# Block sums of the mixing matrix made in DRAM by copies and adding transfers, and weight pieces split three steps earlier, in a two-layer attention and gMLP kernel

## The chip, the cores and the metric

The kernel runs on one core of a Trainium2 chip. The metric is the device time of one execution in microseconds. The core has engines with queues of their own: TensorE (PE; its weight loads are shown as PEld), VectorE (DVE), ScalarE (ACT), GpSimd (POOL) and SyncE (SP), which here issues every transfer. Sixteen transfer engines move data between DRAM, where inputs, output and scratch tensors lie, and the on-chip memory.

## The reference

Two pairs of layers run over x (2048 rows of 512). The first of a pair is linear attention with 32 heads of 16, the second a gMLP block whose mixing matrix w_sp (2048 x 2048) mixes rows:

```python
x = x + A(layernorm(x)); x = x + B(layernorm(x)); x = x + A(layernorm(x)); x = x + B(layernorm(x))

def A(x, wqkv, wo):      # per head, phi(t) = where(t > 0, t + 1, exp(t)) + 1e-6
    kv = einsum("bhsd,bhse->bhde", phi(k), v);  z = einsum("bhsd->bhd", phi(k))
    return (phi(q) @ kv / (phi(q) . z + 1e-6)) @ wo

def B(x, w_in, w_sp, b_sp, w_out):
    z = gelu(x @ w_in)                       # 1792 wide, halves z1 and z2 of 896
    g = einsum("ts,bsf->btf", w_sp, layernorm(z2)) + b_sp
    return (z1 * g) @ w_out
```

All is float32. The same weights serve both pairs, so w_sp is used twice.

## The kernel before

Every large product runs as three TensorE passes on split operands: `high` (ScalarE) rounds an operand, `low` (VectorE) makes the rest, `mm3` multiplies high by high, high by low and low by high. A matmul has a 128 x 128 weight and 512 columns, or 448 in one product.

Each of two layers L has three stages.

P1 (`P1.run`, steps s = 1 to 17, "the first half" in the short description of the change) goes over 16 row tiles of 128 rows: normalise (`ln_a`, `ln_b`), turn by a round trip through DRAM or by TensorE (`Turn`), the K projection, for s up to 10 the Q projection too (the last six Q tiles come later), phi (`phi`, its last operation on VectorE is L329), and the product `Gmm`, 12 matmuls each. `K_split` (L341) makes the operand of `Gmm`. Beside that, seven pieces of the weight `win2` are split, one a step: `side[0].fetch()` loads a piece from s = 6 on and `side.popleft().piece()` splits it from s = 7 on (to 13), with one ScalarE and one VectorE operation on tiles named bg.

P2 (`P2.run`, steps s = 1 to 18) finishes attention and starts the gMLP. In a step it makes the attention output of a tile (`c`), adds it to x, takes row statistics (`stats`: VectorE sums, then three small POOL operations L200, L201, L203), normalises (ScalarE, L209), stores and reloads the tile turned (tensors yt; qt is the same for queries), projects it onto win2 (`e`, 24 matmuls of 448 columns), and projects groups of four tiles onto win1 (`f`, stored to DRAM as z1). `w1.piece(True)` splits pieces of win1, with the low part on POOL, in the first steps.

P4 (`P4.run`) applies w_sp by a Strassen-like scheme of seven products in the order P2, P1, P6, P7, P4, P5, P3, each in 8 steps k over blocks (56 steps g in all, 24 matmuls in a step of P2, P1, P4 and P5, 18 in the others; lines L902 to L904). Step g calls `fetch(g + 4)`, which loads its w_sp blocks, two 128 x 512 sheets, into a quad buffer, and `sp(g + 2)`, which splits them (L840 on ScalarE, L841 on VectorE). P6, P7, P5 and P3 use not blocks of w_sp but sums of blocks. With a21, a22, a11, a12 for four sheets of one (k, j) there are four sums: s1 = a21 + a22, s3 = a21 + a11, s2 = s1 + a11, s4 = s2 + a12. They are the same in both layers, so they are made once, in layer 0, and kept in DRAM: `Sums.s[m, k]`, a pair of sheets j = 0, 1.

Class `Sums` makes them in 32 ticks of two POOL adds each (L782). A tick stores the sheets of the tick before (`store`, L777), loads sheets for the next (`fetch`, three or one of them, L115 through `load`), and adds. Four ticks run in P1 of layer 0 (steps 2 to 5, in sheets cut from two big buffers by class `Sheets`), the others in P2 from step 6 on and in P4 up to step 15 (`if s > 5: sums.tick()`, `if g < 16: self.sums.tick()`). In layer 1 there is nothing left to do for a tick. All loads and stores go through SP's queue in program order; a store that waits for its data holds those behind it. The order of every queue is written out by hand: it is the order of the calls.

Of the kernel before, what the change touches and what calls it, by code (L numbers as in the profile page):

```python
# [10 lines left out]
F32 = mybir.dt.float32  # L11
# [4 lines left out]
P = 128  # L16
# [13 lines left out]
class Slots:  # L30


    def __init__(self, pool, prefix, n):
        self.pool, self.prefix = pool, prefix
        self.free_list = deque(range(n))
        self.held = {}
        self.count = 0
# [9 lines left out]
    def put(self, *tiles):  # L47
        for t in tiles:
            n, _ = self.held.pop(id(t))
            self.free_list.append(n)  # L50


class Sheets:


    def __init__(self, slots, n):
        self.slots = slots
        self.tiles = [slots.get([P, NF, 512]) for _ in range(n)]
        self.free_list = deque(t[:, f, :] for t in self.tiles for f in range(NF))

    def get(self, shape):
        return self.free_list.popleft()

    def put(self, *sheets):
        self.free_list.extend(sheets)

    def close(self):
        self.slots.put(*self.tiles)


@with_exitstack
def mixer_kernel(ctx: ExitStack, tc: tile.TileContext, x_in, wqkv, wo_d, win1_d, win2_d, wsp_d, bsp_d, wout_d,
# [192 lines left out]
    class P1:  # L265
# [163 lines left out]
        def run(self, sums):  # L429
            side = deque([self.win2] * NF)  # L430
            ND = NT - DEFER
            for s in range(1, NT + 2):
                self.loadx(s + 3)
                self.turn.load(s + 1)
                if 2 <= s < NT:
                    self.T_high(s)
                if s == 1:
                    if not self.kb:
                        self.K(0)
                    self.K(1)  # L440
                elif 2 < s <= NT:
                    self.K(s - 1)
                self.ln_a(s + 2)
                if 2 <= s < NT:
                    self.T_low(s)
                if s <= NT:
                    self.K_phi(s - 1)
                if s <= ND:
                    self.Q(s - 1)
                if s == NT + 1:  # L450
                    self.late()
                if s <= NT:
                    self.xsplit(s - 1)
                    self.K_split(s - 1)
                self.ln_b(s + 2)
                if s <= ND:
                    self.Q_phi(s - 1)
                if s >= 2:
                    self.Gmm(s - 2)
                if s == NT + 1:  # L460
                    self.late_phi()
                if self.L == 0 and s == 2:
                    sums.slots = Sheets(bigs, 2)
                if self.L == 0 and 2 <= s < 6:
                    sums.tick(s < 5)
                if self.L == 0 and s == 6:
                    sums.store()
                    sums.slots.close()
                    sums.slots = pages
                if s == 6:  # L470
                    self.wv, self.wo = (quads.get([P, 4, 512]) for _ in range(2))
                    nc.sync.dma_start(self.wv, wqkv[:, 1024:1536].rearrange("(c p) f -> p c f", p=P))
                    nc.sync.dma_start(self.wo, wo_d.rearrange("(c p) f -> p c f", p=P))
                if s > 6 and side:
                    side.popleft().piece()
                if s > 5 and side:
                    side[0].fetch()


# [62 lines left out]
    class P2:  # L542
# [152 lines left out]
        def run(self, sums):  # L695
            w1 = self.win1
            for s in range(1, NT + 3):
                self.loadx(s + 1)
                self.qturn.load(s + 1)
                if s in self.qturn.by_pe:  # L700
                    self.c(s - 1)
                    self.b_high(s)
                    self.c2(s - 1)
                    self.b_low(s)
                    if s >= 2:
                        self.d_high(s - 2)
                        self.d_low(s - 2)
                    self.p1.late()
                    self.c3(s - 1)
                    self.a2(s + 2)  # L710
                    self.p1.late_phi()
                    self.a(s + 3)
                else:
                    if s < NT:
                        self.b_high(s)
                    self.a2_den(s + 2)
                    if s < NT:
                        self.b_low(s)
                    if s <= NT:
                        self.c(s - 1)  # L720
                        self.c2(s - 1)
                    if s == NT:
                        quads.put(*self.W2)
                        pages.put(self.zbc)
                    self.a2_mul(s + 2)
                    late = s - 2 in self.xturn.by_pe
                    if late:
                        self.d_high(s - 2)
                        self.d_low(s - 2)
                    if s <= NT:  # L730
                        self.c3(s - 1)
                    self.a(s + 3)
                    if s <= NT + 1 and not late:
                        self.d_high(s - 2)
                        self.d_low(s - 2)
                if s >= 4:
                    self.e4(s - 4)
                self.xturn.load(s - 1)
                if s >= 3:
                    self.e(s - 3)  # L740
                    self.e2(s - 3)
                    self.e3(s - 3)
                self.f()
                self.f()
                self.fq.extend(self.fnext)
                self.fnext = []
                w1.piece(True)
                w1.fetch()
                if s > 5:
                    sums.tick()  # L750
                if s >= NT + 1:
                    self.p4.fetch(s - NT - 1)
            self.e4(NT - 1)
            self.win2.free()


    class Sums:

        def __init__(self):
            self.s = {(m, k): dram.tile([P, 2, 512], F32, name=f"s{m}_{k}") for m in range(1, 5) for k in range(HT)}
            self.todo = deque((k, j, h) for k in range(HT) for j in range(2) for h in range(2))
            self.ahead = deque(self.todo)
            self.raw, self.made, self.done = {}, [], []
            self.slots = pages

        def fetch(self):
            if self.ahead:
                k, j, h = self.ahead.popleft()  # L770
                at = ((j, k), (j, k + HT), (2 + j, k)) if h == 0 else ((2 + j, k + HT),)
                self.raw.setdefault((k, j), []).extend(load(wsp_d[n, s], self.slots) for n, s in at)

        def store(self):

            for m, k, j, t in self.made:
                nc.sync.dma_start(self.s[m, k][:, j, :], t)  # L777
            self.slots.put(*self.done)
            self.made, self.done = [], []

        def add(self, m, k, j, t, a, b):
            nc.gpsimd.tensor_tensor(t, a, b, op=OP.add)  # L782
            self.made.append((m, k, j, t))

        def tick(self, ahead=True):
            self.store()
            if not self.todo:
                return
            if not self.raw:
                self.fetch()  # L790
            if ahead or self.todo[0][2] == 0:
                self.fetch()
            k, j, h = self.todo.popleft()
            if h == 0:
                a21, a22, a11 = self.raw[k, j][:3]
                self.add(1, k, j, a22, a21, a22)
                self.add(3, k, j, a21, a21, a11)
                self.done = [a21]
            else:
                _, a22, a11, a12 = self.raw.pop((k, j))  # L800
                self.add(2, k, j, a11, a22, a11)
                self.add(4, k, j, a12, a11, a12)
                self.done = [a22, a11, a12]


    class P4:
# [15 lines left out]
        def fetch(self, g):  # L822
            if g >= len(self.steps):
                return
            p, k = self.steps[g]
            t = quads.get([P, 2, 512])
            if p in ("P1", "P2", "P4"):
                n, s = {"P1": (2, k), "P2": (2, k + HT), "P4": (0, k + HT)}[p]
                nc.sync.dma_start(t, wsp_d[n:n + 2, s].rearrange("j p t -> p j t"))
            else:  # L830
                nc.sync.dma_start(t, self.sums.s[{"P6": 2, "P7": 3, "P5": 1, "P3": 4}[p], k])
            self.raw[g] = t

        def sp(self, g):
# [169 lines left out]
        def run(self, nxt):  # L1004
# [10 lines left out]
            for g in range(n):  # L1015
# [6 lines left out]
                if evac_first:  # L1022
                    self.evac(p)
                    self.sp(g + 2)
                if g < 16:
                    self.sums.tick()
                if g == 3:
                    self.loadb()
# [86 lines left out]
```

## Time and profile before

| | us |
|---|---|
| median of 3 runs | 1404.9 (1404.71 to 1405.46) |
| the profiled execution | 1404.73 |
| its span, first to last instruction | 1402.9 |
| busy in the span: TensorE, VectorE, ScalarE, POOL | 1389.6, 886.4, 561.0, 405.6 |

The page of the profile gives busy times by engine, the chain of work that ended last, and groups of instructions by line, each with count, busy time, mean length and idle time of the engine just before it, with what ended that. Other views group by stretches of time ("windows": busy time and count of each engine, granted TensorE clock, share of the 16 transfer engines in use, GB/s), list waits by who waited for whom, or list instructions in order of time. A matmul's row lasts longer than the interval to the next, since they overlap. The granted clock is 1.00 throughout. Line numbers are those of the kernel before.

These groups are POOL's largest, beside the two that the prediction shows: the gates of P4 (L929, 85.5 us), the running sum of phi(k) (L346, 48.8 us), and the three operations of the row statistics (L200, L201, L203: 36.4, 54.8 and 27.2 us).

### The profile page before, as it was taken

Reading aid. Unit: us, or ns where it says so; the run is one execution under the profiler, and the core shown is the slowest. Engines: PE = TensorE matmul, PEld = TensorE weight load, DVE = VectorE, ACT = ScalarE, POOL = GpSimd, SP = SyncE. Lnnn points to the kernel's source line nnn. Section 1 sums busy time; section 2 is a strip of 40 time slices with the busy share of each in tenths; the row PEclk is TensorE's granted clock in tenths of the full one; section 3 lists DMA queues with packets and bytes.
Section 4 is the critical chain, followed back from the end, with each engine's and each line's share of the span. In section 5 each row is a group of like instructions: output and inputs, shape, how many; then the busy total and the mean of one; then the engine's idle time right before and its main releaser. Section 6 shows DMA issues by size and latency. Waiting matters only on the chain.

```text
span 1402.9 us, 17320 instructions
## 1 busy us (share of the span) xinstructions
PE 1389.6 (99%) x6230; PEld 1156.7 (82%) x6230; DVE 886.4 (63%) x1251; ACT 561.0 (40%) x847; POOL 405.6 (29%) x490
## 2 busy tenths in 40 slices
PE   9999999999999999999999999999999999999998
PEld 7877788888888888888788778888888888888887
DVE  7786777752577666573577867766415466665632
ACT  5564534434323332341356645444333233333420
POOL 4644345544365002040023434432100030022300
PEclk9999999999999999999999999999999999999999
DMA  5842267876897433443635413555334344334432
GB/s 176 270 142 62 73 192 237 271 228 207 305 326 248 134 120 135 173 158 120 210 101 184 129 46 99 179 179 162 114 116 158 104 165 134 133 117 167 155 110 94
DMA packets 142263, 225.69 MB, mean 161 GB/s; under 512 B 11744, under 2 KB 50400, under 8 KB 142176
## 3 DMA queue, kind: packets, MB, share of 16 engines
q1 hardware_dynamic: 142176, 224.57, 48.6%
q8 instruction: 49, 0.80, 0.2%
q14 instruction: 38, 0.31, 0.1%
HBM read 156.63 MB, written 67.90 MB: 160 GB/s over the span
## 4 chain that ended last, share of the span: by engine, by line
PE 87%; DVE 6%; ACT 4%; issue 1%; DMA 1%; POOL 0%; SPq 0%; DVEq 0%; ACTq 0%; POOLq 0%
PE bank L135 15%; PE bank L134 15%; PE bank L133 15%; PE bank L902 13%; PE bank L904 13%; PE bank L903 13%; DVE pg L260 1%; DVE pg L341 1%; DVE pg L329 1%; ACT pg L328 1%; DMA pg<-in_win_dram 1%; ACT pg L327 1%; PE bank L515 1%; PE bank L526 0%; PE bank L221 0%
## 5 line engine op out<-in xcount | busy, mean ns | idle before, releaser
L902 PE MATMUL bank<-qd,pg 128*128 128x512 f32 x800 | 311.2, 389 | 0.0
L904 PE MATMUL bank<-qd,pg 128*128 128x512 f32 x800 | 311.2, 389 | 0.0
L903 PE MATMUL bank<-qd,pg 128*128 128x512 f32 x800 | 311.2, 389 | 0.0
L841 DVE TENSOR_TENSOR qd<-qd,qd 128x1024 fp32r<-128x1024 f32 x112 | 151.8, 1355 | 178.7 <-ACT qd L840 174.2
L840 ACT ACTIVATE qd<-qd 128x1024 fp32r<-128x1024 f32 x112 | 118.5, 1058 | 215.7 <-PE bank L904 199.0
L929 POOL TENSOR_TENSOR bg<-bg,pg 128x512 f32<-128x512 f32 x56 | 85.5, 1564 | 409.7 <-DVE bg L956 195.5
L904 PEld LDWEIGHTS bank<-qd,pg 128*128 128x128 f32 x800 | 150.2, 188 | 31.3
L903 PEld LDWEIGHTS bank<-qd,pg 128*128 128x128 f32 x800 | 150.2, 188 | 31.2
L902 PEld LDWEIGHTS bank<-qd,pg 128*128 128x128 f32 x800 | 150.1, 188 | 31.1
L135 PE MATMUL bank<-qd,pg 128*128 128x512 f32 x384 | 150.7, 392 | 2.5 <-DVE pg L122 2.5
L200 POOL TENSOR_SCALAR rs<-mv 128x1 f32<-128x1 f32 x96 | 36.4, 379 | 384.4 <-DVE mv L198 377.2
L209 ACT ACTIVATE pg<-pg,nb,rs 128x512 f32<-128x512 f32 x63 | 51.1, 811 | 181.6 <-POOL nb L203 175.5
L133 PE MATMUL bank<-qd,pg 128*128 128x512 f32 x288 | 112.4, 390 | 0.0
L134 PE MATMUL bank<-qd,pg 128*128 128x512 f32 x288 | 112.3, 390 | 0.0
L782 POOL TENSOR_TENSOR pg<-pg,pg 128x512 f32<-128x512 f32 x56 | 81.5, 1456 | 47.7 <-DMA pg<-in_wsp_dram 41.8
L133 PE MATMUL bank<-bg,qd 128*128 128x448 f32 x256 | 94.1, 368 | 0.0
L135 PE MATMUL bank<-bg,qd 128*128 128x448 f32 x256 | 93.7, 366 | 0.1
L134 PE MATMUL bank<-bg,qd 128*128 128x448 f32 x256 | 93.6, 366 | 0.0
L135 PEld LDWEIGHTS bank<-qd,pg 128*128 128x128 f32 x384 | 72.0, 188 | 20.8 <-DVE pg L122 6.0
L135 PE MATMUL bank<-wo,qd 128*128 128x512 f32 x224 | 87.3, 390 | 0.8 <-DVE qd L122 0.8
L133 PE MATMUL bank<-wo,qd 128*128 128x512 f32 x224 | 87.3, 390 | 0.7 <-ACT qd L119 0.7
L135 PE MATMUL bank<-qd,bg 128*128 128x512 f32 x224 | 87.4, 390 | 0.0
(121 smaller groups left out, 2571.7 us busy)
## 6 DMA issues: line engine op xcount, KB each, us to landing
qd<-s SPq DMA_DIRECT2D x64, 512.0 KB, 3.4
qd<-in_wsp_dram SPq DMA_DIRECT2D x48, 512.0 KB, 3.8
pg<-x SPq DMA_DIRECT2D x64, 256.0 KB, 2.9
z<-pg SPq DMA_DIRECT2D x56, 256.0 KB, 2.5
pg<-in_wsp_dram SPq DMA_DIRECT2D x56, 256.0 KB, 5.0
s<-pg SPq DMA_DIRECT2D x56, 256.0 KB, 4.8
pg<-z SPq DMA_DIRECT2D x56, 256.0 KB, 5.4
x<-pg SPq DMA_DIRECT2D x48, 256.0 KB, 2.6
```

The source lines that it names most:

```text
L133: nc.tensor.matmul(out, ah, bh, start=start, stop=False)
L134: nc.tensor.matmul(out, ah, bl, start=False, stop=False)
L135: nc.tensor.matmul(out, al, bh, start=False, stop=stop)
L200: nc.gpsimd.tensor_scalar(rs, mv[:, 1:2], LN_EPS, None, op0=OP.add)
L209: nc.scalar.activation(y, x, AF.Identity, bias=nb, scale=rs)
L782: nc.gpsimd.tensor_tensor(t, a, b, op=OP.add)
L840: nc.scalar.activation(w[:, 0], r, AF.Copy)
L841: nc.vector.tensor_sub(w[:, 1], r, w[:, 0].bitcast(F32))
L902: m(out, h[:, o], w[:, 0, j, :], start=start, stop=False, skip_group_check=True)
L903: m(out, h[:, o], w[:, 1, j, :], start=False, stop=False, skip_group_check=True)
L904: m(out, l[:, o], w[:, 0, j, :], start=False, stop=stop, skip_group_check=True)
L929: nc.gpsimd.tensor_tensor(u, u, z1, op=OP.mult)
```

## The change

`Sums` no longer loads sheets into on-chip memory. The sums lie in DRAM as `s[m, j, k]`, two sheets for an even k (k and k + 1) of one j, 512 KB each, 32 such tensors in eight groups (j, k). For each, SP issues a copy within DRAM of the first block ("c"), and later POOL issues a transfer within DRAM that adds the second block, or the sum made before, onto it ("a"). `PLAN` gives the tick within a group: c1 and c3; a1 and c2; a3 and c4; a2; nothing; a4. A group starts every second tick, so there are 20 ticks, with three copies and one add in an even tick and one copy and three adds in an odd one. As built, a copy is cut into 16 rows of 8192 elements and an add into 128 rows of 1024. An add waits for its copy, and a2 and a4 also for the sum that they read (a1 and a2, two ticks earlier).

Ticks run in P2 from step 3 to 18 and in P4 from step 0 to 7 (of which four have something to do), and none in P1. `Sheets` and the POOL adds are gone. `P4.fetch` reads a pair of sums in two transfers of 256 KB, where there was one of 512 KB. In P1 of both layers the pieces of win2 are fetched from step 3 and split from step 4 (to 10).

```diff
@@ P1.run
-                if self.L == 0 and s == 2:
-                    sums.slots = Sheets(bigs, 2)
-                if self.L == 0 and 2 <= s < 6:
-                    sums.tick(s < 5)
-                if self.L == 0 and s == 6:
-                    sums.store()
-                    sums.slots.close()
-                    sums.slots = pages
...
-                if s > 6 and side:
+                if s > 3 and side:
                     side.popleft().piece()
-                if s > 5 and side:
+                if s > 2 and side:
                     side[0].fetch()
@@ P2.run
-                if s > 5:
+                if s > 2:
                     sums.tick()
@@ Sums
+        GROUPS = [(j, k) for k in range(0, HT, 2) for j in range(2)]
+        PLAN = ("c1", "c3"), ("a1", "c2"), ("a3", "c4"), ("a2",), (), ("a4",)
+
         def __init__(self):
-            self.s = {(m, k): dram.tile([P, 2, 512], F32, name=f"s{m}_{k}") for m in range(1, 5) for k in range(HT)}
-            self.todo = deque((k, j, h) for k in range(HT) for j in range(2) for h in range(2))
...
+            self.s = {(m, j, k): dram.tile([2, P, 512], F32, name=f"s{m}_{j}_{k}")
+                      for m in range(1, 5) for j, k in self.GROUPS}
+            n, p = len(self.GROUPS), len(self.PLAN)
+            self.todo = deque([(g, x) for g in range(n) if 0 <= t - 2 * g < p for x in self.PLAN[t - 2 * g]]
+                              for t in range(2 * n + p - 2))
+
+        def tile(self, m, j, k):
+            return self.s[m, j, k - k % 2][k % 2]
+
+        def tick(self):
             if not self.todo:
                 return
...
+            for g, (what, m) in self.todo.popleft():
+                j, k = self.GROUPS[g]
+                m = int(m)
+                out = self.s[m, j, k]
+                own, k0 = {1: (j, k), 3: (j, k), 2: (2 + j, k), 4: (2 + j, k + HT)}[m]
+                if what == "c":
+                    nc.sync.dma_start(out, wsp_d[own, k0:k0 + 2])
+                else:
+                    n, s = (j, k + HT) if m == 1 else (2 + j, k)
+                    src = wsp_d[n, s:s + 2] if m % 2 else self.s[m // 2, j, k]
+                    nc.gpsimd.dma_start(out, src, accum_op=OP.add, max_dma_last_dim=4096)
@@ P4.fetch
-                nc.sync.dma_start(t, self.sums.s[{"P6": 2, "P7": 3, "P5": 1, "P3": 4}[p], k])
+                for j in range(2):
+                    nc.sync.dma_start(t[:, j, :], self.sums.tile({"P6": 2, "P7": 3, "P5": 1, "P3": 4}[p], j, k))
@@ P4.run
-                if g < 16:
+                if g < 8:
                     self.sums.tick()
```

More of the change, by code (lines that the diff above doesn't have):

```diff
@@ L50, in put @@
             self.free_list.append(n)
[L53 to L68, printed above, removed]
 @with_exitstack
@@ L757, in mixer_kernel @@
     class Sums:
+        GROUPS = [(j, k) for k in range(0, HT, 2) for j in range(2)]
+        PLAN = ("c1", "c3"), ("a1", "c2"), ("a3", "c4"), ("a2",), (), ("a4",)
         def __init__(self):
-            self.s = {(m, k): dram.tile([P, 2, 512], F32, name=f"s{m}_{k}") for m in range(1, 5) for k in range(HT)}
-            self.todo = deque((k, j, h) for k in range(HT) for j in range(2) for h in range(2))
-            self.ahead = deque(self.todo)
-            self.raw, self.made, self.done = {}, [], []
@@ L766, in __init__ @@
[L766 to L786, printed above, removed]
+            self.s = {(m, j, k): dram.tile([2, P, 512], F32, name=f"s{m}_{j}_{k}")
[3 more added lines that the diff above has]
+                              for t in range(2 * n + p - 2))
@@ L787, in tick @@
+        def tile(self, m, j, k):
+            return self.s[m, j, k - k % 2][k % 2]
+        def tick(self):
             if not self.todo:
                 return
[L789 to L803, printed above, removed]
+            for g, (what, m) in self.todo.popleft():
[9 more added lines that the diff above has]
+                    nc.gpsimd.dma_start(out, src, accum_op=OP.add, max_dma_last_dim=4096)
```

## The prediction

> **What bounds the kernel now.** I read the page first: busy shares, the chain of waits, the costliest groups.
>
> ```profile
> span 1402.9 us, 17320 instructions
> PE 1389.6 (99%) x6230; PEld 1156.7 (82%) x6230; DVE 886.4 (63%) x1251; ACT 561.0 (40%) x847; POOL 405.6 (29%) x490
> ...
> PE 87%; DVE 6%; ACT 4%; issue 1%; DMA 1%; POOL 0%; SPq 0%; DVEq 0%; ACTq 0%; POOLq 0%
> ...
> L902 PE MATMUL bank<-qd,pg 128*128 128x512 f32 x800 | 311.2, 389 | 0.0
> ...
> L782 POOL TENSOR_TENSOR pg<-pg,pg 128x512 f32<-128x512 f32 x56 | 81.5, 1456 | 47.7 <-DMA pg<-in_wsp_dram 41.8
> ```
>
> TensorE sets the time: busy 1389.6 of 1402.9 us, never idle ahead of the mixing matmuls (L902, last column 0.0). Taking work off POOL therefore buys nothing directly. Idle TensorE is 13.3 us in all; further pauses hide in its overlapping rows, so matmuls are counted too. The view by stretches shows where, and how full the transfer engines are (last two columns: share of the 16 engines, GB/s):
>
> ```profile
> core 0: us, PE busy (x) PEld busy (x) DVE busy (x) ACT busy (x) POOL busy (x), PEclk, DMA share, GB/s
> 60.00:95.00 35.00, 35.00 (x156) 28.98 (x155) 27.36 (x39) 22.40 (x39) 13.69 (x20) 1.00 0.62 199
> 95.00:125.00 30.00, 28.04 (x118) 21.24 (x117) 25.01 (x32) 18.07 (x31) 11.73 (x12) 1.00 0.33 96
> 790.00:825.00 35.00, 33.61 (x145) 26.53 (x145) 27.19 (x34) 19.54 (x33) 12.68 (x12) 1.00 0.32 98
> 173.00:345.00 172.00, 171.94 (x796) 148.56 (x795) 111.91 (x175) 70.00 (x114) 86.15 (x128) 1.00 0.70 225
> 868.40:1040.40 172.00, 172.00 (x798) 149.23 (x797) 102.12 (x176) 71.29 (x115) 50.91 (x101) 1.00 0.47 150
> 360.00:420.00 60.00, 60.00 (x266) 49.69 (x265) 43.56 (x43) 17.95 (x24) 35.53 (x23) 1.00 0.98 337
> ```
>
> At full rate (60 to 95) 156 matmuls start in 35.00 us, one in 0.224 us. In 95 to 125 only 118 start, where 134 could: 16 x 0.224 = 3.5 us lost. In 790 to 825 it is 156 - 145 = 11: 2.5 us. These are the last steps of P1 in the two layers. P2 (fourth and fifth row, the same stretch of layer 0 and layer 1, the second without sums) loses nothing, but its transfers differ: 0.70 against 0.47.
>
> **Part 1: the pieces of win2 leave steps 11 to 13.** VectorE's timeline:
>
> ```profile
> 94.03 0.69 DVE L329 SCALAR_TENSOR_TENSOR pg<-bank,pg 128x512 f32<-128x512 f32 x1 [0.39 <-ACT pg L328]
> ...
> 100.48 0.69 DVE L329 SCALAR_TENSOR_TENSOR pg<-bank,pg 128x512 f32<-128x512 f32 x1 [0.46 <-ACT pg L328]
> ...
> 103.40 0.68 DVE L122 TENSOR_TENSOR bg<-pg,bg 128x512 fp32r<-128x512 f32 x1
> ...
> 106.94 0.69 DVE L329 SCALAR_TENSOR_TENSOR pg<-bank,pg 128x512 f32<-128x512 f32 x1 [0.46 <-ACT pg L328]
> ...
> 113.38 0.69 DVE L329 SCALAR_TENSOR_TENSOR pg<-bank,pg 128x512 f32<-128x512 f32 x1 [0.39 <-ACT pg L328]
> ...
> 119.23 0.69 DVE L329 SCALAR_TENSOR_TENSOR pg<-bank,pg 128x512 f32<-128x512 f32 x1 [0.46 <-ACT pg L328]
> ```
>
> From L329 to L329 is a step: 6.46 and 6.44 us with a piece (the 0.68 us row writing bg), 5.85 without. A late step has no Q, so TensorE needs 24 x 0.224 = 5.4 us: VectorE sets the pace. Three pieces out of it: 3 x 0.68 = 2.0 us a layer, 4.1 us in both (step 5.85 still exceeds 5.4, so some of the 6.0 us lost stays). In steps 4 to 6 a piece arrives where TensorE needs 36 x 0.224 = 8.1 us and VectorE's step with a piece is about 7.4 (86.65 to 94.03):
>
> ```profile
> 86.65 0.69 DVE L329 SCALAR_TENSOR_TENSOR pg<-bank,pg 128x512 f32<-128x512 f32 x1 [0.45 <-ACT pg L328]
> ```
>
> So it lies under the matmuls; without that cover three pieces cost the 2.0 us back per layer. The chain of waits also shows how late they may be:
>
> ```profile
> 58.74 8.89 DMA pg<-in_win_dram
> ```
>
> It stands 8.89 us on the load of the first piece, and TensorE pauses nowhere (60 to 95 is full). The new fetch comes one step ahead, without the sums' loads in front of it. I take -4.1 us; bounds -6.0 and 0.
>
> **Part 2: the sums as transfers.** Removed: 64 POOL adds of 1.46 us, with 64 loads and 64 stores of 256 KB (32 MB), in 32 ticks over P1, P2 and P4. They delayed no matmul, so they return nothing. Added: 32 copies of 512 KB from SP and 32 adding transfers of 512 KB from POOL, in 20 ticks, 16 of them at the end of P2's steps 3 to 18 of layer 0, the rest in P4's steps 0 to 3. By the plan, P2 gets 16 (c1, c3) + 8 (c2) + 7 (c4) = 31 copies and 8 + 7 + 7 + 6 = 28 adds.
>
> The room: P2's other transfers are those of layer 1, 0.47 x 172 = 81 us of all 16 engines (0.70 x 172 = 120 with today's sums), so 91 us are free.
>
> The price of a copy: none in DRAM at both ends is in the trace. The nearest row is the fullest stretch, 360 to 420: 337 / 0.98 = 344 GB/s, so 524 KB / 344 = 1.52 us. Twice that, 3.05, is the other end, if read and write in one memory go one after the other; nothing allows a gain. I take 1.52, for every transfer of the trace has a reading and a writing end too. The price of an add: it must read the addend and the old sum and write once. Low end one pass, 1.52; high end three passes at the dear copy's half, 4.57; I take two passes, 3.05, since two streams come in.
>
> Sum: 31 x 1.52 + 28 x 3.05 + 81 = 47 + 85 + 81 = 213 us in 172: 41 too many. Not all of it reaches TensorE. A P2 step is 12.0 us:
>
> ```profile
> 224.62 1.29 POOL L561 TENSOR_TENSOR pg<-z_q,pg 128x512 f32<-128x512 f32 x1
> ...
> 236.58 1.29 POOL L561 TENSOR_TENSOR pg<-z_q,pg 128x512 f32<-128x512 f32 x1
> ```
>
> x, qt and yt are fetched a step ahead of use (12 us), an add waits for a copy of the tick before or an add two ticks back, and nothing reads the sums until P4's third product, so about another step of backlog can stand: 24 us absorbed, an estimate. 41 - 24 = 17 us reach TensorE.
>
> Who is late: on SP's queue, behind one copy in odd ticks and three in even ones (with c4), stand the loads of x and qt for the next steps, the stores of qt, x and yt, the load of yt, the z1 stores. On POOL, behind an add that waits for its copy or its predecessor, stands the next L200 (the row's variance), then L203, for which ScalarE's L209 waits already:
>
> ```profile
> POOL rs L200 <- DVE mv L198: 377.2, 89, 34.9
> ...
> ACT pg L209 <- POOL nb L203: 175.5, 36, 22.0
> ```
>
> POOL has 377 us of waiting to give there, ScalarE 175 us; behind L209 come the stores of yt, the projection onto win2, and TensorE.
>
> The Trainium skill, DMA: Bandwidth & Descriptors, section Latency and other measured facts, gives 214 GB/s per direction as the full rate of copies between HBM tensors. No run here shows it yet. A copy would take an estimated 2.45 us by it, and the forecast below would grow by 31 x 0.93 = 29 us from the copies alone.
>
> POOL's own time for issuing: no row shows it. SP's issues of the same data bound it:
>
> ```profile
> L115 SPq DMA_DIRECT2D pg<-in_wsp_dram x56: 333/456/1661, 203.2 to 425.2; - x56
> ```
>
> 0.33 to 1.66 us, so three adds in an odd tick cost POOL 1.0 to 5.0 us. POOL is busy 86 of 172 us in P2, 6 of 12 us a step, 2.9 of it the adds that leave: it is hidden. Beyond about 2.9 us an add it would delay L200 directly.
>
> **Part 3: the sums are read by two transfers of 256 KB, not one of 512 KB,** in both layers.
>
> ```profile
> L831 SPq DMA_DIRECT2D qd<-s x64: 319/320/440, 418.3 to 1303.5; - x64
> ...
> DMA to landing us min/median/max: 2.3/3.6/7.2
> ```
>
> 64 more issues of 0.32 us, at most one in each P4 step of at least 4.1 us (18 matmuls x 0.224), four steps ahead of use: nothing, and if the lead were gone 64 x 0.32 = 20 us. That P4's 0.98 stretch loses most of its sums is worth nothing either: TensorE is full there (60.00 of 60.00).
>
> Sum: the profiled execution took 1404.73 us (span 1402.9 and 1.8 around it), 0.2 below the median of 1404.9. 1404.73 - 4.1 + 17 = 1418 us.
>
> **The rivals.**
> 1. The adds cost one pass (two streams read side by side): 59 x 1.52 = 90 us, 171 in all of 172, hidden; Part 1 stays: 1404.73 - 4.1 = 1400.6 us. For it: P4 runs at 0.98 with full matmuls. Against: P2's loads have one step of lead where P4's have four.
> 2. Copies and adds at the dear ends: 31 x 3.05 + 28 x 4.57 + 81 = 304, 132 too many, 108 after 24: 1404.73 - 4.1 + 108 = 1508 us. For it: both ends in the one memory. Against: at 0.98 nothing slows below 337 GB/s.
> 3. The excess is just absorbed and eats the gain: adds of about 2.2 us give 190 us, 18 over, under the 24; a few transfers late for 2 to 6 us in the first, shorter steps pay Part 1 back: 1403 to 1407 us.
> 4. Part 1 doesn't do what it says, because 5.85 us or ScalarE keeps the late steps as long: with hidden transfers 1404.7 us. VectorE's rows speak against it.
>
> The Trainium skill, Collectives: The Full Stack, Part 3, says that a reducing transfer emits two reading descriptors per chunk on one ring and so runs at half a copy's rate. No run here shows it yet; by it rival 1 falls and the add is the one that I took.
>
> **How the numbers follow.** Forecast 0.42; rival 1 0.36; rival 2 0.12; rivals 3 and 4 together 0.10. About 0.2% (2.8 us) is what a measurement of this kernel can tell from no change. Faster: rival 1, 0.36. Same: rivals 3 and 4, 0.10. Slower: 0.42 + 0.12 = 0.54. The likeliest case's own range is 1405 to 1460 us (from adds of 2.6 us beside copies of 1.52, to adds of 3.6 beside copies of 2.4). The range that holds 8 of 10 takes in rival 1 with the full 6.0 us (1398) and the cheaper part of rival 2: 1398 to 1470.
>
> **What would show it.** Right: in P2 of layer 0 the share is near 1.0 and TensorE has idle time ahead of L133 to L135 that ends in DVE or ACT rows, behind POOL or yt; the stretch to the first mixing matmul is some 17 us longer; VectorE's late P1 steps fall to 5.9 us. Wrong: P2 still 172 us long, with copies and adds landing within a step; or POOL's issues of an add above 2.9 us, which would put the loss on POOL, not on the transfer engines; or a loss in P4, which I cost at nothing.

## The result, and the profile after

| | us |
|---|---|
| before, median of 4 runs | 1405.18 (1404.71 to 1405.79) |
| after, median of 4 runs | 1449.43 (1442.93 to 1451.28) |
| after / before | 1.0306, 95% interval 1.0274 to 1.0339 |
| the profiled execution after (its span) | 1449.89 (1448.1) |

The change makes the kernel 44 us slower. The forecast said slower, but by 13 us; the time lies inside the range, which was drawn wide for other costs of a copy and an add. In the page of the kernel after, the busy shares, the transfer queues and the chain of waits answer to the lines shown of before:

```profile
span 1448.1 us, 17195 instructions
PE 1402.2 (97%) x6230; PEld 1166.1 (81%) x6230; DVE 857.7 (59%) x1251; ACT 562.3 (39%) x847; POOL 343.0 (24%) x458
...
q1 hardware_dynamic: 133984, 207.79, 43.7%
q0 software_dynamic: 4608, 16.78, 6.6%
...
PE 75%; DMA 12%; DVE 7%; ACT 3%; issue 2%; POOL 1%; SPq 0%; DVEq 0%; ACTq 0%; POOLq 0%
```

POOL lost 63 us of work, as meant. TensorE is no longer busy throughout (span less busy is 45.9 us, where it was 13.3), and transfers have gone from 1% to 12% of the chain. "Software" is the queue of POOL's transfers, here the adds alone; "hardware" is SP's.

The view by stretches of the kernel after, same columns as before, tells the stages apart (first three rows: P1 of layer 0, full part and late steps, and the late steps of layer 1; then P2 of layer 0, first 172 us and the last 55):

```profile
60.00:95.00 35.00, 35.00 (x156) 28.96 (x155) 27.99 (x39) 23.54 (x40) 13.69 (x18) 1.00 0.50 162
95.00:125.00 30.00, 29.72 (x129) 23.79 (x128) 23.81 (x28) 15.71 (x27) 11.76 (x12) 1.00 0.28 80
836.00:871.00 35.00, 34.77 (x152) 27.97 (x151) 26.78 (x33) 18.88 (x33) 12.76 (x12) 1.00 0.27 83
173.00:345.00 172.00, 149.97 (x650) 127.20 (x649) 89.11 (x153) 56.29 (x92) 61.81 (x103) 0.92 0.92 255
345.00:400.00 55.00, 42.48 (x182) 35.98 (x181) 12.00 (x21) 16.13 (x26) 14.07 (x25) 0.88 0.88 226
```

The late steps of P1 start 129 matmuls instead of 118, and 152 instead of 145. P2 of layer 0 starts 650 where it started 796, at a share of the transfer engines of 0.92 instead of 0.70, and the granted clock is 0.92 and 0.88 instead of 1.00. From the first matmul of each stage in the two traces, in us:

| stage | before | after | difference |
|---|---|---|---|
| P1, layer 0 | 133.5 | 131.1 | -2.4 |
| P2, layer 0 | 222.4 | 269.5 | +47.1 |
| P4, layer 0 | 272.1 | 274.4 | +2.4 |
| P1, layer 1 | 201.0 | 199.1 | -1.9 |
| all else | 573.9 | 574.0 | +0.1 |

(Each stage runs from its first matmul to the next stage's; that of P1 in layer 1 begins with the output product of layer 0.) So the whole question is P2 of layer 0. The list of waits of the kernel after, over the whole run:

```profile
POOL rs L182 <- DVE mv L180: 451.6, 92, 35.0
...
DVE pg L242 <- DMA pg<-yt: 60.0, 11, 18.0
...
PE bank L115 <- ACT qd L101: 34.7, 7, 12.5
```

L115 is TensorE's L133 of before, L242 the turn of the loaded yt, L101 `high`, L182 the first small operation of the row statistics, L97 SP's loads (L115 before). POOL isn't late: L182 still waits 451.6 us for VectorE. The turned rows are: VectorE waits 60.0 us for the load of yt (before 3.1), and seven times TensorE stands for it. What SP's queue itself waited for, in the stretch from 160 to 440 us, is the next view. Before:

```profile
SPq L115 <- DMA yt<-pg: 24.7, 12, 2.9
```

After:

```profile
SPq L97 <- DMA yt<-pg: 102.6, 12, 18.0
```

The load of yt is queued behind a wait for its store to land, and everything that SP issues later is queued behind that load. One of the longest of these waits, in order of time on SP's and POOL's queues of the kernel after:

```profile
226.78 0.78 SPq L594 DMA_DIRECT2D x<-pg  x1
227.66 0.47 SPq L227 DMA_DIRECT2D yt<-pg  x1
...
232.54 1.80 POOL L761 DMA_DIRECT2D s<-s  x2 [0.17 <-issue]
...
233.73 1.45 POOL L761 DMA_DIRECT2D s<-in_wsp_dram  x1
...
245.79 0.32 SPq L97 DMA_DIRECT2D pg<-yt  x1
```

The store of yt goes out at 227.66 and its load at 245.79: the store took 18.1 us where 2.5 us was the median of the yt transfers before, and SP issued nothing in those 18 us. Three adds, issued five to six microseconds after the store, landed before it (240.3, 243.1 and 245.6 us by the trace's landing times). Then, in order of time over all engines:

```profile
243.02 0.39 PE L117 MATMUL bank<-qd,pg 128*128 128x512 f32 x1
...
248.69 1.08 DVE L242 STREAM_TRANSPOSE pg<-pg 128x512 f32<-128x512 f32 x1 [7.89 <-DMA pg<-yt]
249.80 0.63 ACT L101 ACTIVATE qd<-pg 128x512 fp32r<-128x512 f32 x1 [7.05 <-DVE pg L242]
...
250.48 0.74 PE L115 MATMUL bank<-bg,qd 128*128 128x448 f32 x1 [7.07 <-ACT qd L101]
251.02 0.57 PE L116 MATMUL bank<-bg,qd 128*128 128x448 f32 x1
251.40 0.57 PE L117 MATMUL bank<-bg,qd 128*128 128x448 f32 x1
...
253.62 0.36 PE L117 MATMUL bank<-bg,qd 128*128 128x448 f32 x1
253.82 0.36 PE L115 MATMUL bank<-bg,qd 128*128 128x448 f32 x1
```

TensorE starts no matmul from 243.02 to 250.48. Such stalls come at every second step, the one with three adds. Beyond the stall, the matmuls behind it start 0.37 us apart until 253.62, then 0.20: the view by short stretches shows the granted clock doing it.

```profile
238.00:244.00 6.00, 5.41 (x24) 4.13 (x22) 2.73 (x6) 0.82 (x1) 2.64 (x4) 1.00 1.03 205
244.00:250.00 6.00, 0.00 (x0) 0.00 (x0) 1.08 (x1) 0.20 (x1) 0.00 (x0) 0.73 0.86 237
250.00:256.00 6.00, 5.52 (x20) 4.88 (x21) 3.73 (x7) 3.34 (x6) 1.93 (x4) 0.70 0.68 218
256.00:262.00 6.00, 6.00 (x29) 5.04 (x28) 3.02 (x7) 0.92 (x2) 2.56 (x4) 1.00 1.01 255
```

Counted over 160 to 460 us by the intervals between matmul starts, less the usual interval of each shape: eight pauses of 0.7 us or more hold 37.0 us, six of them in P2 (5.0, 7.2, 2.6, 6.7, 1.3 and 12.7: 35.5 us) and two in P4. Seventy smaller excesses hold 12.7 us; 63 of these, 11.5 us, stand where the granted clock is 0.50. Together 49.7, against 47.1 + 2.4 in the table; P2's share is 35.5 + 11.5 = 47.0.

Last, who used the engines while the store of yt was out. The transfer view of the kernel after from 240 to 246 us (packets, MB, share of 16 engines):

```profile
q0 software_dynamic: 242, 0.86, 72.3%
q1 hardware_dynamic: 121, 0.06, 4.6%
```

The adds held 72% of the engines and SP's queue 4.6%, though the store was the older transfer. An add's packet of 4096 bytes lasts 327 ns, one of the store's 512 bytes 27 ns, by the trace's packet records.

### The profile page after: what moved, and what is told of

Its sections match the earlier page's. It is cut to its first block, busy times and chain, and to the rows that moved or that the text cites. A ratio compares the mean times of both kernels' runs of the same rounds, so it can differ in the third digit from the quotient of the medians.

```text
span 1448.1 us, 17195 instructions
## 1 busy us (share of the span) xinstructions
PE 1402.2 (97%) x6230; PEld 1166.1 (81%) x6230; DVE 857.7 (59%) x1251; ACT 562.3 (39%) x847; POOL 343.0 (24%) x458
## 4 chain that ended last, share of the span: by engine, by line
PE 75%; DMA 12%; DVE 7%; ACT 3%; issue 2%; POOL 1%; SPq 0%; DVEq 0%; ACTq 0%; POOLq 0%
PE bank L117 12%; PE bank L863 12%; PE bank L116 12%; PE bank L861 12%; PE bank L115 12%; PE bank L862 12%; DMA yt<-pg 6%; DMA pg<-yt 3%; DMA qd<-in_wsp_dram 1%; DVE pg L242 1%; DVE pg L323 1%; DVE st L178 1%; DVE pg L556 1%; PE bank L489 0%; DVE pg L311 0%
## 5 line engine op out<-in xcount | busy, mean ns | idle before, releaser
L182 POOL TENSOR_SCALAR rs<-mv 128x1 f32<-128x1 f32 x96 | 36.5, 380 | 452.0 <-DVE mv L180 451.6
L115 PE MATMUL bank<-bg,qd 128*128 128x448 f32 x256 | 99.6, 389 | 34.5 <-ACT qd L101 34.5
L242 DVE STREAM_TRANSPOSE pg<-pg 128x512 f32<-128x512 f32 x75 | 81.0, 1080 | 81.1 <-DMA pg<-yt 60.0
L115 PE MATMUL bank<-qd,pg 128*128 128x512 f32 x288 | 112.3, 390 | 0.0
L116 PE MATMUL bank<-bg,qd 128*128 128x448 f32 x256 | 98.0, 383 | 0.0
L117 PE MATMUL bank<-bg,qd 128*128 128x448 f32 x256 | 97.9, 382 | 0.1
L115 PE MATMUL bank<-wo,qd 128*128 128x512 f32 x224 | 87.3, 390 | 0.2 <-ACT qd L101 0.2
```

The lines of the kernel that those rows point to most:

```text
L115: nc.tensor.matmul(out, ah, bh, start=start, stop=False)
L116: nc.tensor.matmul(out, ah, bl, start=False, stop=False)
L117: nc.tensor.matmul(out, al, bh, start=False, stop=stop)
L182: nc.gpsimd.tensor_scalar(rs, mv[:, 1:2], LN_EPS, None, op0=OP.add)
L242: nc.vector.transpose(y.rearrange("p c (t m) -> p m c t", m=4), r.rearrange("p (m c j) -> p m c j", m=4, c=4))
```

## The experiments

Three theories are set against each other; the third was added after e4. Volume: P2 of layer 0 is asked for 213 us of the engines in 172, and the rest comes out as time. Bursts: three adds at once keep the engines for some 9 us. Turns: SP's small packets take turns with the adds' long ones, so that a store lasts as long as the long packets between its own. Each run was compared with runs of the kernel before on the same chip, at medians of 1405.0 to 1405.5 us. Diffs are against the kernel named.

**e1, the pieces alone** (the kernel before, with Part 1's edit only):

```diff
-                if s > 6 and side:
+                if s > 3 and side:
...
-                if s > 5 and side:
+                if s > 2 and side:
```

> The kernel before with the pieces of win2 fetched from step 3 and split from step 4, sums as before. If the working of Part 1 holds, it is 4.1 us faster than before (3 to 5). If ScalarE or the step of 5.85 us keeps the late steps as long, within 1 us of before.

1404.29 us, ratio 0.9994 (0.9985 to 1.0003): a miss. Stretches of e1:

```profile
60.00:95.00 35.00, 35.00 (x153) 28.21 (x152) 28.11 (x40) 22.01 (x38) 12.51 (x17) 1.00 0.63 202
95.00:125.00 30.00, 28.64 (x119) 21.74 (x119) 24.34 (x30) 18.13 (x31) 13.04 (x15) 1.00 0.27 74
```

In layer 0 three matmuls are lost in 60 to 95 and only one is won in 95 to 125; P1 takes 133.9 us. In layer 1, where no tick runs beside P1, it gained 1.6 us. ScalarE's row of a piece in e1 names what it waited for:

```profile
69.45 0.63 ACT L119 ACTIVATE bg<-pg 128x512 fp32r<-128x512 f32 x1 [3.50 <-DMA pg<-in_win_dram]
```

Its late steps are 5.9 us long, as forecast (VectorE's L329 at 96.0, 101.9, 107.8 and 113.8 us), but they begin 2.0 us later than before (94.0): the early pieces took in layer 0 what the late steps gave. The change also takes the ticks, with their loads, out of P1, and got the gain. No run takes the ticks out of P1 and leaves the pieces late, so how layer 0's gain divides between the two isn't shown.

**e2, two adds and two adds** (after; a4 moved by a tick, so that no tick has more than two adds):

```diff
-        PLAN = ("c1", "c3"), ("a1", "c2"), ("a3", "c4"), ("a2",), (), ("a4",)
+        PLAN = ("c1", "c3"), ("a1", "c2"), ("a3", "c4"), ("a2",), (), (), ("a4",)
```

> The changed kernel with a4 one tick later in the plan, so that every tick has two adds instead of three and one; the same transfers in the same steps. Volume theory (213 us of transfers do not fit in 172 us of P2, however they lie): about the changed kernel's time, 1440 to 1455 us. Burst theory (three adds at once delay yt in the odd steps): the loss falls by half or more, under 1428 us.

1453.57 us, ratio 1.0345 (1.0326 to 1.0364). P2 of layer 0 took 270.3 us, as in the kernel after. Bursts of three, as the cause by themselves, fall; bursts of two still stand in it.

**e3, the copies in P1** (after; all 32 copies issued in steps 1 to 16 of P1 of layer 0, the adds where they were):

```diff
+                if self.L == 0:
+                    sums.copies(s)
...
```

> The changed kernel with its 32 copies moved to P1 of layer 0, two a step in steps 1 to 16, the adds where they were. P2 then has 83 us of adds and 81 us of other transfers in 172 us. Volume theory: they fit, 1401 to 1410 us. Burst theory: three adds at once remain in the odd ticks, so a good part of the 45 us remains, over 1418 us.

1418.56 us, ratio 1.0096 (1.0078 to 1.0114). P1 136.4 us, P2 233.1. Moving 47 us of transfers out won back 36 of the 47, but by the prediction's sum 166 us now stand in 172, which should fit, and P2 is still 10.7 us longer than before: over the range of the volume theory, and at the lower end of the burst theory's.

**e4, plain copies in the place of the adds** (after):

```diff
-                    nc.gpsimd.dma_start(out, src, accum_op=OP.add, max_dma_last_dim=4096)
+                    nc.gpsimd.dma_start(out, src, max_dma_last_dim=4096)
```

> The changed kernel with plain copies issued by POOL in place of the adding transfers, same sizes and rows (the sums are then single blocks, not sums). If an add costs two passes, the software queue's share of the 16 engines falls to half, some 47 us in all, and P2 has 171 us of transfers for 172. Volume theory: 1401 to 1412 us. Burst theory: the bursts are half as long, 1401 to 1420 us, with waits left behind the odd ticks.

1420.41 us, ratio 1.0109 (1.0091 to 1.0128); P2 242.2 us. The software queue in e4's page:

```profile
q0 software_dynamic: 4608, 16.78, 3.7%
```

3.7% of its span of 1420.3 us is 52.6 us, 1.64 us for each of 32, against 95.6 / 32 = 2.99 for an add: the adding itself is 1.8 times a copy in the same packets, and leaving it out takes 27 of P2's 47 us away. The time is still over the ranges of both theories: 173 us asked in 172 cost 19.8.

**e5, rows of 1024 bytes for the adds** (after):

```diff
-                    nc.gpsimd.dma_start(out, src, accum_op=OP.add, max_dma_last_dim=4096)
+                    nc.gpsimd.dma_start(out, src, accum_op=OP.add, max_dma_last_dim=1024)
```

> The changed kernel with each add cut into 512 rows of 256 elements instead of 128 of 1024: the same bytes, packets of 1 KB instead of 4 KB. Turns theory (the 16 engines alternate packet by packet between the two queues, so that a 327 ns packet of an add passes for each 28 ns packet of a yt store): yt lands earlier and the loss falls to 1415 to 1435 us. Volume theory: the same work in the engines or more of it for the shorter packets, 1445 to 1475 us; POOL also writes four times the rows.

1435.52 us, ratio 1.0217 (1.0199 to 1.0236). That is just over the turns theory's range and below the volume theory's. The adds now take more of the engines, in e5's page

```profile
q0 software_dynamic: 16896, 16.78, 7.7%
```

which is 110 us against 96, and yet P2 falls from 269.5 to 258.7 us and P4's loss is gone (272.0). The store of yt that took 18.1 us took 15.4 here, and it landed before the second and third add, not after all three. Volume as the only cause of the kernel after falls, since more of it cost 14 us less; shorter packets help, as turns would have it. But a store is still 15 us out, and P2 36 us too long. P2 of layer 0 in e5:

```profile
173.00:345.00 172.00, 152.46 (x657) 128.07 (x656) 90.68 (x156) 56.85 (x92) 66.40 (x106) 0.92 0.99 255
345.00:400.00 55.00, 50.66 (x222) 41.99 (x221) 14.67 (x23) 18.93 (x29) 15.01 (x22) 0.97 1.02 264
```

Now the transfer engines are full (0.99 and 1.02), where in the kernel after they were not (0.92 and 0.88). So volume can account for what is left in e5, but not for all of the loss in the kernel after.

**e6, spread out** (after; one group every fourth tick; ticks in every second step of P1 of layer 0, in every step of P2, and in P4 up to step 11):

```diff
-        PLAN = ("c1", "c3"), ("a1", "c2"), ("a3", "c4"), ("a2",), (), ("a4",)
+        PLAN = ("c1",), ("c3",), ("a1", "c2"), ("c4",), ("a2",), ("a3",), (), ("a4",)
...
+                if self.L == 0 and s % 2 == 0 and s <= 16:
+                    sums.tick()
...
```

> The changed kernel with the same copies and adds spread over 36 ticks, one copy and one add each at most: every second step of P1 in layer 0, every step of P2, then P4's first ten steps. P2 then has 18 x (1.5 + 2.95) = 80 us of sums and 81 of other transfers in some 200 us. Volume theory: hidden, and Part 1 remains: 1400 to 1404 us. If the order on SP's queue alone delays yt, whatever the volume: 1408 to 1425 us.

1409.03 us, ratio 1.0023 (1.0012 to 1.0035). P2 224.8 us: 18 copies and 18 adds, by the plan, ask for 27 + 54 + 81 = 162 us, nearly e3's 165, and cost 2.4 us where e3's bursts cost 10.7. Two cautions: the profiled execution took 1406.0 us, 3 less than the median, so its 2.4 is the cheap end; and e3's transfers are all adds (28), so spacing isn't the only difference. P1 pays too, 134.4 us, as in e1. The time lies in the range of the rival (order on SP's queue), but in the profiled execution P1 loses more (3.3 us, against 131.1) than P2.

**e7, POOL's adds from P2's step 3 on** (the kernel before, no ticks in P1, the pieces early, ticks in P4 up to step 19):

```diff
...
-                if s > 5:
+                if s > 2:
                     sums.tick()
...
-                if g < 16:
+                if g < 20:
```

> The kernel before with its POOL adds, but no ticks in P1 (the first at P2's step 3, the last in P4's step 18), and the pieces of win2 three steps earlier. If the pieces paid in the changed kernel only because P1 had lost its sums, this shows the whole of Part 1: 1400 to 1402 us. If the later ticks cost P2 or P4 something: 1404 us or more.

1404.39 us, ratio 0.9991 (0.9982 to 1.0). P1 of both layers gave what the change gave (131.1 and 198.9 us), and P2 of layer 0 took it back, 226.3 us, in its first steps.

**e8, the copies alone** (after, without the adding transfers):

```diff
-                else:
-                    n, s = (j, k + HT) if m == 1 else (2 + j, k)
-                    src = wsp_d[n, s:s + 2] if m % 2 else self.s[m // 2, j, k]
-                    nc.gpsimd.dma_start(out, src, accum_op=OP.add, max_dma_last_dim=4096)
```

> The changed kernel without its adds (the sums are single blocks). P2 has 47 us of copies and 81 of other transfers in 172. Volume theory: hidden, 1400 to 1404 us. If three copies ahead of the loads on SP's queue delay yt by themselves: 1408 us or more.

1401.29 us, ratio 0.9972 (0.9962 to 0.9982). P2 of layer 0 in e8:

```profile
173.00:345.00 172.00, 171.80 (x791) 147.55 (x790) 100.66 (x172) 69.80 (x113) 49.56 (x98) 1.00 0.77 239
```

At a share of 0.77 TensorE is full, although the store of yt is out for up to 9.2 us: a round trip of that length is hidden. What is left of the change is Part 1, -3.9 us.

**e9, rows of 8192 bytes for the adds** (after):

```diff
-                    nc.gpsimd.dma_start(out, src, accum_op=OP.add, max_dma_last_dim=4096)
+                    nc.gpsimd.dma_start(out, src, accum_op=OP.add, max_dma_last_dim=8192)
```

> The changed kernel with each add cut into 64 rows of 2048 elements: packets of 8 KB, each holding an engine some 0.6 us. Turns theory (yt's short packets wait for an add's packet each): yt later still, 1452 to 1480 us. Volume theory: the adds' total time in the engines is at most what it was (94 us), so 1440 to 1450 us.

1454.79 us, ratio 1.0351 (1.0333 to 1.0368). Packets of 628 ns; the adds take slightly less of the engines (6.4% of the span), P2 272.3 us and P4 279.9. That is more time for less volume, in the direction of turns, but by 5 us only, and the executions of the kernel after lie 8 us apart (1442.93 to 1451.28), those of e9 6: it settles little.

**e10, POOL's adds from P2's step 5 on** (as e7, with `s > 4` in P2 and ticks in P4 up to step 18):

```diff
...
-                if s > 5:
+                if s > 4:
                     sums.tick()
...
-                if g < 16:
+                if g < 19:
```

> The kernel before with its POOL adds, none in P1, the first tick at P2's step 5, the last in P4's step 18, and the pieces of win2 three steps earlier. The early steps of P2, which lost 4 us with ticks at step 3, are left alone: P1 shorter by 2.4 and 2.1 us, 1400 to 1402 us. If the waits move with the ticks: 1403 to 1405 us.

1401.16 us, ratio 0.9967 (0.9954 to 0.998). Stretches of e10:

```profile
60.00:95.00 35.00, 35.00 (x156) 28.98 (x155) 27.98 (x39) 23.43 (x40) 13.67 (x18) 1.00 0.51 164
...
173.00:345.00 172.00, 170.63 (x788) 147.35 (x787) 111.22 (x171) 69.95 (x113) 86.24 (x126) 1.00 0.71 228
```

All of Part 1 with POOL's own adds, by starting them later.

**e11, one copy and one add a tick, from P2 on** (e6's `PLAN`, nothing in P1, ticks in P2 as after and in P4 up to step 19):

```diff
...
-                if g < 8:
+                if g < 20:
```

> The changed kernel with one copy and one add a tick at most, in P2 from step 3 and in P4 to step 19, nothing in P1. P2 then has 16 x (1.5 + 2.95) = 71 us of sums and 81 of other transfers in 172: 0.88 of the engines. If what decides is that they are nearly full: 1402 to 1412 us, with Part 1 in P1 (131.1 us to the first transition matmul). If P4's first steps cannot hide the rest: a loss there, 1408 to 1425 us.

1401.5 us, ratio 0.9974 (0.9965 to 0.9984). P2 of layer 0 in e11:

```profile
173.00:345.00 172.00, 168.97 (x771) 145.16 (x770) 98.62 (x169) 67.03 (x109) 61.17 (x113) 0.99 0.81 225
```

With 16 copies and 13 adds in P2 (24 + 39 + 81 = 144 us asked, 0.84 of 172) nearly all is hidden; the time is just under both ranges. The profiled execution took 1406.23 us, the longest of its eight, so the 227.7 us of its P2 are the dear end. Both e10 and e11 beat the two kernels, the one before by some 4 us; adding transfers and adds on POOL come out alike.

Set beside each other, what P2 of layer 0 was asked for (by the plan and the measured prices), the share of the engines in use from 173 to 345 us, how much longer than 222.4 us P2 took, and the longest yt transfer, in us:

| run | asked | share | longer by | longest yt transfer |
|---|---|---|---|---|
| e5 | 224 | 0.99 | 36.3 | 15.4 |
| after | 211 | 0.92 | 47.1 | 18.6 |
| e9 | 209 | 0.90 | 49.9 | 18.5 |
| e2 | 208 | 0.90 | 47.9 | 16.8 |
| e4 | 173 | 0.89 | 19.8 | 11.6 |
| e3 | 165 | 0.83 | 10.7 | 14.4 |
| e6 | 162 | 0.87 | 2.4 | 8.1 |
| e11 | 144 | 0.81 | 5.3 | 11.6 |
| e8 | 128 | 0.77 | 0.8 | 9.2 |

The loss starts under 172 and follows no column alone: e5 asks for more than the kernel after and loses less, and e3 loses more than e6 at nearly the same volume and a lower share.

## Why the prediction came out as it did

**Part 1** was right in size: 4.3 us in the two layers against 4.1, and VectorE's late steps in the kernel after are 5.9 us:

```profile
99.13 0.69 DVE L311 SCALAR_TENSOR_TENSOR pg<-bank,pg 128x512 f32<-128x512 f32 x1 [0.53 <-ACT pg L310]
...
116.84 0.69 DVE L311 SCALAR_TENSOR_TENSOR pg<-bank,pg 128x512 f32<-128x512 f32 x1 [0.46 <-ACT pg L310]
```

(three steps in 17.7 us). In layer 1 the pieces alone give it (e1, 1.6 us). In layer 0 they alone gave nothing (e1), and with the ticks out of P1 the whole (e10): the condition that the forecast named, no loads of the sums in front of the pieces, carries that share.

**The prices of Part 2** were right. A copy: the 512 packets of 32 KB took 48.0 us of all 16 engines, 1.50 us each, forecast 1.52; so close is in part luck, since the same copies took 1.40 in e5 and 1.73 in e8. An add: 2.99, forecast 3.05. So the 213 us asked and the 41 too many stand (211 and 39 by the measured prices). The Trainium skill's rate for copies between HBM tensors (DMA: Bandwidth & Descriptors, Latency and other measured facts), an estimated 2.45 us a copy, isn't borne out by these contiguous copies: the measurement decides. The Trainium skill's two reads for a reducing transfer (Collectives: The Full Stack, Part 3) agree with e4 against the kernel after, 1.8 times.

**POOL's issuing** was rightly hidden. The two groups of adds in the kernel after, with the shortest, median and longest issue in ns:

```profile
L761 POOL DMA_DIRECT2D s<-in_wsp_dram x16: 912/1085/1767, 181.4 to 386.6; - x16
L761 POOL DMA_DIRECT2D s<-s x16: 812/942/1152, 203.0 to 418.3; - x16
```

The medians, some 1 us, are inside the bounds; the longest, 1.77, is just over them and below the 2.9 at which L182 would have been late. POOL waited for a transfer of the sums three times (28.4 us), all from 388 us on, at the end of P2 and in P4.

**The step that failed** is "24 us absorbed". It credited one step of lead and one of backlog, 12 us each, against the excess of 41. On balance nothing was absorbed: P2 grew by 47.1 us, 35.5 in pauses and 11.5 in slow matmuls. That the pauses come near the excess of 39 to 41 proves nothing, since the engines weren't full while time was lost (0.92 x 172 + 0.88 x 55 = 207 us in 227), and e3 lost 10.7 us at 165 us asked, with room to spare.

The lead isn't 12 us. In the kernel before, in order of time over all engines:

```profile
237.50 0.37 SPq L245 DMA_DIRECT2D yt<-pg  x1
...
240.07 0.32 SPq L115 DMA_DIRECT2D pg<-yt  x1
...
247.41 1.07 DVE L260 STREAM_TRANSPOSE pg<-pg 128x512 f32<-128x512 f32 x1
```

The load landed at 243.03 by the trace's landing times, 4.4 us before VectorE turns it (2.4 to 4.8 us in eleven of the twelve such steps of layer 0, none in the last). Store, landing, load and turn stand one behind the other and fill most of a step, so a store that takes 18.1 us instead of 2.5 is late by far. The backlog isn't there either: while the store is out SP issues nothing, neither loads nor copies, and SP's queue stood 102.6 us for such stores from 160 to 440 us, 24.7 in the kernel before.

**A term was missing**: the granted clock after a pause, 11.5 us in P2. And P4, costed at nothing, lost 2.4 us. In the stretch from 400 to 470 us of the kernel after the waits name it:

```profile
ACT qd L799 <- DMA qd<-in_wsp_dram: 10.8, 3, 4.8
```

The loads of w_sp blocks come while the last copies and adds are still under way; that they are held up by these isn't shown by itself. The sums' split reads (Part 3) cost nothing, since in e8 and e11 they are the same and P4 takes 272.0 and 272.7 us. In all, -4.3 + 35.5 + 11.5 + 2.4 = 45.1 us, and the two profiled executions are 45.2 apart.

**What made the store late** is partly settled. That the adds delay it is shown (e8: without them 9.2 us at most and no loss). That packet length matters beside volume is shown by e5. The Trainium skill (DMA: Bandwidth & Descriptors, Queues, rings and completion order) says that each engine goes round the queues and drains a whole packet before switching; 72.3% against 4.6% from 240 to 246 us agrees in kind. But the records of packets don't name the engine, and what the page calls a packet needn't be one record of the trace, so the turns themselves aren't seen.

The packet records divide the 18.1 us of the store shown. Its 512 packets of 512 bytes and as many of the store of qt before it begin 6.3 us after its issue, behind the copies and loads that SP had queued. Of these 1024 packets the last 100 take 5.0 us, beside the adds. At the same store the last 100 take 5.0 us in e5 too, where the adds' packets are a quarter of the size, and 9.1 in e9, where they are twice the size. So turns row by row don't explain what e5 gained. How the 47 us divide between volume, bursts and turns stays open, and so does what spacing is worth by itself, since e3 and e6 differ in their number of adds too.

## What to carry to other kernels

Add up the engine time of the transfers stage by stage and compare it with what is free there; but allow slack only where no round trip through the same engines stands inside each step, since a store that must land before the next load stops the whole queue behind it. Spread transfers that add, one to a step, over more stages, rather than pack them: e11 did both, and lost almost nothing. Before moving work off an engine with 377 us of waiting, try only to start it later: with the pieces early, that (e10) won as much as the best form of the transfers.

## What the runs showed of the hardware

- After a pause of TensorE the granted clock is half for a while. Two stretches of the kernel after, behind a pause of 7.2 us and one of 2.6:

```profile
247.00:253.00 6.00, 2.52 (x7) 2.12 (x8) 2.86 (x4) 3.01 (x5) 0.00 (x0) 0.50 0.92 263
281.00:284.00 3.00, 3.00 (x9) 2.36 (x8) 1.69 (x4) 2.47 (x5) 0.26 (x2) 0.50 1.03 407
```

  Matmuls then start 0.36 to 0.54 us apart instead of 0.20; behind the pause of 7.2 us that cost some 1.5 us, in P2 11.5 us in all. The Trainium skill (TensorE: Matmul & The Clock Gate, Part 1) has the clock halve after an idle window of about 3.4 us and return after a busy one; 0.37 against 0.20 for the 3.1 us to 253.62 agrees. Here the pause of 2.6 us was enough, and the one of 1.3 us at 341 us was not.
- A transfer within DRAM that adds costs 1.8 times a copy in the same packets (2.99 and 1.64 us for 512 KB), and 1024-byte rows cost some 15% more than 4096-byte ones (110 and 96 us for 32).
- A copy in DRAM in 32 KB packets keeps the 16 engines busy for 1.50 us per 524 KB in the kernel after, 350 GB/s, about the rate of the fullest stretch of loads before (344); the other runs give 1.40 to 1.73 us.
